# Windowed attention feeding a convolution-gated two-layer network: global rows' scores issued product by product, some elementwise work moved between engines, and a new order of the whole program

## Chip, cores, metric

One NeuronCore of a Trainium2 chip runs the whole problem in a single launch. The metric is device time in microseconds. In the profile PE is TensorE (matmuls), PEld its weight loads, DVE is VectorE, ACT is ScalarE, POOL is GpSimd, and SP is SyncE, which here only issues DMAs.

## What is computed

```python
# 8 batches, 8 heads, 512 local and 32 global rows, head size 64
k_all = concat([k_g, k_l]); v_all = concat([v_g, v_l])
out_g = softmax(0.125 * q_g @ k_all.T) @ v_all           # global rows see all rows
s_ll  = where(|i - j| <= 32, 0.125 * q_l @ k_l.T, -1e9)  # local rows: window of 32 ...
s_lg  = 0.125 * q_l @ k_g.T                              # ... and the global rows
out_l = softmax(concat([s_lg, s_ll])) @ concat([v_g, v_l])
x = concat([out_g, out_l]) as [8 batches, 544 rows, 512]
h = relu(x @ w_in)                                       # 512 -> 1024
c = 3-tap convolution of h along the rows, weights conv_w
out = (h * sigmoid(c)) @ w_out                           # 1024 -> 512
```

## The kernel before

**Attention.** Two heads share the 128 partitions. For each of the 32 pairs of heads, `SC` makes the scores of both (32 products of 32 by 128 on line 258, fp32), and then each head goes alone through: `MA` on VectorE (mask added in PSUM, line 288; row maximum, line 289), `NM` (the maximum scaled, line 238 or 240), `EX` on ScalarE (four exponentials with their sums, line 301), `NS` on VectorE (reciprocal of the sums, lines 317 and 318), `NP` (division of the probabilities, lines 324 to 326) and `TD` on VectorE (32 by 32 transposes, line 311). `PV` multiplies by the values (line 352), `UA` copies the result out of PSUM (line 357), `XW` writes it to a DRAM tile `row` (line 363). Once per batch come the global rows: `G` (24 products on line 282), `GM`, `GE`, `GN`, `GS` (softmax), `GT` and `GC` (transposes and their copies), `GP`, `GO`, `GW`.

`G` is what the change rewrites. For each of four pairs c it makes a product of 384 columns, one of 128 and one of 32, each for the two halves j of the partitions (one head in each half). The pair c fixes the 32 output partitions, c * 32 to c * 32 + 32. The rewritten loop has the same 24 products. In the trace each fp32 product of this kind leaves two matmul records.

**The network.** The 4360 columns of `row` (8 batches of 545) are cut into nine chunks of 484 or 486 columns. For each chunk, `XR` reads four tiles back (line 370), `XH` and `XL` split each into a high part (ScalarE cast, line 205) and a low part (a subtraction, line 208) that suit TensorE's fp32r format. `Z` makes one of eight hidden tiles with 12 products (line 468; three for each of the four x tiles in turn: high, low, high). Each hidden tile is then worked through `RE` (relu, line 476), `C1` (first tap, line 240 when GpSimd does it), two more taps `Ca`, `Cb` on VectorE (line 487), `TH` (tanh, line 494), `GG` (line 498), and again a split into `GH` (cast, line 205) and `GL` (difference, line 208). `O` makes four output tiles with two times 12 products each (line 522), `OE` copies one out, `ST` stores it. A chunk can begin only when the attention of its batch is written and read back.

**Weights.** `w_in` and `w_out` come as 64-bit floats in eight pieces of 1 MB and are turned into fp32 bit by bit: `WA` on ScalarE (line 107), `WC` on VectorE (four instructions, lines 114, 115, 118, 192), `WH` on ScalarE (high part), `WL` on VectorE (low part, line 208).

**What sets the order.** Nothing in the program is issued in the order in which it is written here. A planner (`plan`, `in_time`, `arranged`) gives each step a cost per engine and a due time from the tables `POS`, `POS0`, `POS1` and `TIME`, lists all steps by engine, and `emit` issues them in that order; each engine then runs its own list strictly in order and waits by semaphores. `ENG0` says which engine does a step in the first phase (attention of batches 0 and 1, chunk 0, weights), `ENG` which does it later: "a" is ScalarE, "v" VectorE, "p" GpSimd. The pools' sizes are in `SLOTS`: eight PSUM banks, four tiles of keys, two hidden tiles `h` and two `t`.

Of the kernel before, what the change touches and what calls it, by code (L numbers as in the profile page):

```python
# [64 lines left out]
def attn_moe(ctx: ExitStack, tc: tile.TileContext, qk_d, vw_d, qg_d, w_in_d, w_out_d, cw_d, out_d):  # L65
    nc = tc.nc
# [196 lines left out]
    def G(n):  # L263
# [302 lines left out]
    LQ=40.87, LG=215.93, LV=-243.12, S=107.44, M=-70.51, E=5.13, NS=-78.62, NM=29.46, P=56.84, UA=-17.62,  # L566
    XW=130.55, XR=1.62, NP=66.53, TD=36.03, XH=3.06, XL=-78.47, G=116.57, GM=-316.88, GE=52.46, GN=-126.8,
    GS=36.17, GT=-9.45, GC=-378.84, GP=142.18, GO=60.71, GW=-40.85, PZ=150.79, RE=268.18, C1=145.08, Ca=-140.4,
    Cb=-113.5, TH=59.26, GG=-47.92, GH=-6.62, GL=-138.03, Oa=147.2, Ob=58.82, OE=35.95, ST=218.68, WD=203.65,
    WA=218.1, WC=-74.47, WH=335.66, WL=135.18,  # L570
# [8 lines left out]
POS1 = dict(
    LQ=-63.39, LG=301.35, LV=-335.85, S=193.3, M=77.03, E=20.47, NS=-248.75, NM=-259.8, P=113.29, UA=-43.88,  # L580
    XW=-158.89, XR=-54.07, NP=-38.76, TD=-137.17, XH=-242.78, XL=-129.5, G=-35.21, GM=-113.52, GE=137.51,
    GN=-160.66, GS=-99.25, GT=71.36, GC=-144.02, GP=-27.71, GO=-126.33, GW=45.2, PZ=-196.53, RE=160.59,
    C1=-347.5, Ca=-48.32, Cb=3.66, TH=302.11, GG=61.24, GH=-381.31, GL=-125.69, Oa=6.05, Ob=-16.32, OE=-249.32,
    ST=-157.23, WD=-338.43, WA=368.5, WC=-177.51, WH=182.59, WL=368.35,
# [3 lines left out]
    A0=131.07, R0=-90.01, A1=-373.5, R1=272.56, A2=429.96, R=151.66, PER=64.94, T0=274.61, Z0=-174.31,  # L588
    O0=267.42, OR0=-83.25, T1=275.17, ZR=-32.34, OD=-0.43, OR=-1.06, END=285.22,
# [8 lines left out]
def cost(key, e):  # L598
# [380 lines left out]
```

## Time and profile before

| | us |
|---|---|
| median of 3 runs | 592.79 |
| lowest and highest run | 589.4, 593.7 |
| the profiled execution | 589.3 |
| its span, first to last instruction | 587.5 |

The span is what the views of the profile divide up; 1.8 us of the execution's time lie around it. Every duration below comes from this one execution. Busy times count an engine's instructions, not its waits; the chain of waits says at each moment what the last instruction was waiting for.

### The profile page before, as it was taken

How to read it: one execution, taken by the hardware profiler on the slowest of the kernel's cores; microseconds unless marked ns; L12 is line 12 of the kernel's file. 1: busy time of each engine (PE TensorE's matmuls, PEld its weight loads, DVE VectorE, ACT ScalarE, POOL GpSimd, SP SyncE). 2: the span in 40 equal slices, each digit the busy share in tenths (PEclk: the TensorE clock that was granted, in tenths of full speed). 3: DMA queues.
4: the chain of work that ended last, by engine and by line, in shares of the span. 5: the costliest groups of instructions: out<-in, count | busy, mean ns of one | idle time of the engine just before them, and what ended most of it. 6: DMA issues, size and time to landing. Idle time of an engine off the chain costs nothing.

```text
span 587.5 us, 19573 instructions
## 1 busy us (share of the span) xinstructions
PE 541.6 (92%) x8208; PEld 449.7 (77%) x8208; DVE 406.5 (69%) x846; ACT 391.3 (67%) x1296; POOL 65.4 (11%) x113
## 2 busy tenths in 40 slices
PE   4573599999997999999999999999999999999997
PEld 3362377878786878787888788878888888888886
DVE  4689899999775648876868665758667864552560
ACT  4944896877574888788649965897579753432431
POOL 3000111111120001100200110011100101110110
PEclk9596599999998999999999999999999999999999
DMA  8769662740427416711556027703310230111101
GB/s 352 288 242 304 260 213 79 222 125 35 126 89 203 178 40 175 232 66 39 151 152 223 17 68 198 259 18 120 92 36 29 97 122 0 52 51 35 34 2 67
DMA packets 34984, 74.75 MB, mean 127 GB/s; under 512 B 9808, under 2 KB 21584, under 8 KB 33872
## 3 DMA queue, kind: packets, MB, share of 16 engines
q1 hardware_dynamic: 34896, 73.50, 38.3%
q8 instruction: 64, 1.05, 0.7%
q14 instruction: 24, 0.20, 0.1%
HBM read 55.65 MB, written 17.84 MB: 125 GB/s over the span
## 4 chain that ended last, share of the span: by engine, by line
PE 83%; DVE 7%; issue 5%; DMA 2%; ACT 2%; SPq 1%; POOL 0%; DVEq 0%; ACTq 0%; POOLq 0%
PE ps_h L468 32%; PE ps_o L522 32%; PE ps_v L352 7%; PE psg L282 5%; PE ps_s L258 4%; PE go L438 2%; DMA qk<-qk 1%; ACT pr L301 1%; PE gt L423 1%; DMA raw<-w_out 1%; DVE t L487 1%; DVE negm L289 1%; DVE wt L118 1%; DVE xl L208 1%; DVE nt L205 1%
## 5 line engine op out<-in xcount | busy, mean ns | idle before, releaser
L468 PE MATMUL ps_h<-xh,w_in 128*128 128x486 f32 (+1 forms) x576 | 191.4, 394 | 10.4 <-ACT pr L301 10.1
L522 PE MATMUL ps_o<-g,w_out 128*128 128x484 f32 (+1 forms) x864 | 200.1, 385 | 0.1
L522 PEld LDWEIGHTS ps_o<-g,w_out 128*128 128x128 f32 x864 | 162.3, 190 | 28.4 <-issue 1.6
L468 PEld LDWEIGHTS ps_h<-xh,w_in 128*128 128x128 f32 x576 | 110.2, 191 | 32.5 <-ACT pr L301 10.9
L487 DVE SCALAR_TENSOR_TENSOR t<-h,cw,t 128x484 f32<-128x484 f32 (+1 forms) x144 | 102.5, 721 | 34.6 <-POOL t L240 33.7
L468 PE MATMUL ps_h<-xl,w_in 128*128 128x486 f32 (+1 forms) x288 | 112.0, 389 | 3.1 <-DVE xl L208 3.1
L240 POOL TENSOR_SCALAR t<-h,cw 128x484 f32<-128x484 f32 (+1 forms) x72 | 57.7, 802 | 435.9 <-ACT h L476 307.1
L301 ACT ACTIVATE pr<-ps_s,negm 128x128 f32<-128x128 f32 x256 | 90.3, 378 | 1.8 <-POOL negm L240 1.3
L324 ACT ACTIVATE pr<-pr,sums 128x128 f32<-128x128 f32 x256 | 80.5, 407 | 2.9 <-DVE sums L317 2.0
L498 DVE SCALAR_TENSOR_TENSOR t<-t,h 128x484 f32<-128x484 f32 (+1 forms) x72 | 48.9, 685 | 26.3 <-ACT t L494 26.1
L352 PEld LDWEIGHTS ps_v<-pt,vf 32*64 32x64 f32 x3328 | 48.8, 133 | 21.0 <-issue 14.9
L468 PEld LDWEIGHTS ps_h<-xl,w_in 128*128 128x128 f32 x288 | 55.0, 191 | 12.1 <-DVE xl L208 4.0
L352 PE MATMUL ps_v<-pt,vf 32*64 32x64 f32 (+3 forms) x3328 | 53.8, 245 | 10.8 <-issue 10.3
L476 ACT ACTIVATE h<-ps_h 128x486 f32<-128x486 f32 (+1 forms) x72 | 42.0, 583 | 27.2 <-PE ps_h L468 25.5
L208 DVE TENSOR_TENSOR g<-t,g 128x484 fp32r<-128x484 f32 (+1 forms) x72 | 47.5, 666 | 15.6 <-ACT g L205 14.8
L494 ACT ACTIVATE t<-t 128x484 f32<-128x484 f32 (+1 forms) x72 | 43.6, 612 | 20.1 <-DVE t L487 20.0
L301 ACT ACTIVATION_READ_ACCUMULATOR pr<-ps_s,negm 128x1 f32 x256 | 55.9, 219 | 0.0
L205 ACT CAST g<-t 128x484 fp32r<-128x484 f32 (+1 forms) x72 | 42.9, 600 | 16.0 <-DVE t L498 15.6
L311 DVE STREAM_TRANSPOSE pt<-pr 128x512 f32<-128x512 f32 x64 | 43.3, 695 | 14.8 <-ACT pr L324 12.6
L258 PE MATMUL ps_s<-qk 64*32 64x128 f32 x2048 | 39.5, 295 | 14.7 <-issue 9.3
L258 PEld LDWEIGHTS ps_s<-qk 64*32 64x32 f32 x2048 | 31.9, 113 | 21.5 <-issue 12.8
L289 DVE TENSOR_REDUCE negm<-ps_s 128x4 f32<-128x512 f32 x64 | 44.3, 692 | 3.3
(63 smaller groups left out, 388.0 us busy)
## 6 DMA issues: line engine op xcount, KB each, us to landing
qk<-qk SPq DMA_DIRECT2D x32, 704.0 KB, 5.8
vf<-vw SPq DMA_DIRECT2D x32, 448.0 KB, 4.8
row<-nt SPq DMA_DIRECT2D x32, 256.0 KB, 4.1
xl<-row SPq DMA_DIRECT2D x24, 243.0 KB, 4.0
raw<-w_in SPq DMA_DIRECT2D x4, 1024.0 KB, 11.5
raw<-w_out SPq DMA_DIRECT2D x4, 1024.0 KB, 8.3
xl<-row SPq DMA_DIRECT2D x8, 244.0 KB, 3.3
out<-o SPq DMA_DIRECT2D x4, 242.0 KB, 2.1
```

The source lines that it names most:

```text
L205: nc.scalar.copy(out=out, in_=in_) if choice(key) == "a" else eng(key).tensor_copy(out=out, in_=in_)
L208: eng(key).tensor_tensor(out=out, in0=in0, in1=in1, op=ALU.subtract)
L240: nc.gpsimd.tensor_scalar(out=out, in0=in_, scalar1=by, scalar2=0.0, op0=ALU.mult, op1=ALU.add)
L258: nc.tensor.matmul(heads[n + j]["s"][b * SG : (b + 1) * SG, t].rearrange("p (a b k) -> p a b k", a=2, b=2), lhsT=qk[rows, at : at + SG], r ...
L289: nc.vector.tensor_reduce(out=st["m"], in_=st["s"], axis=mybir.AxisListType.X, op=ALU.max)
L301: nc.scalar.activation(out=st["p"][:, t, :], in_=st["s"][:, t, :], func=AF.Exp, scale=SCALE, bias=st["m"][:, t : t + 1], accum_out=two["r" ...
L324: nc.scalar.activation(out=p[:, t], in_=p[:, t], func=AF.Copy, scale=r[:, t : t + 1])
L352: nc.tensor.matmul(x, lhsT=v, rhs=p, start=k == 0, stop=k == len(work[j, b]) - 1)
L468: nc.tensor.matmul(st["z"][:, 0:n], lhsT=w[:, ft, ct, :], rhs=x, start=i == 0, stop=i == 3 * NCT - 1)
L487: nc.vector.scalar_tensor_tensor(out=st["t"], in0=st["h"][:, k : k + n], scalar=cw[:, 3 * ft + k : 3 * ft + k + 1], in1=st["t"], op0=ALU.m ...
L498: nc.vector.scalar_tensor_tensor(out=t, in0=t, scalar=1.0, in1=h, op0=ALU.add, op1=ALU.mult)
L522: nc.tensor.matmul(ps, lhsT=w[:, mt, ft, :], rhs=g, start=ft + i == 0, stop=ft == NFT - 1 and i == 2)
```

## The change

Three things change. The products of `G` come in another order: first all 384-column ones over the four pairs, then all of 128 columns, then all of 32, so that neighbours differ in their output partitions. Steps change engine: in the first phase `NP` goes from ScalarE to GpSimd, `NM` from GpSimd to ScalarE, `C1` from GpSimd to ScalarE, `UA`, `GS`, `GO` and `OE` from VectorE to ScalarE, `GC` from ScalarE to VectorE; later `C1` goes from GpSimd to ScalarE, `XL` from VectorE to GpSimd, `GH` and `OE` from ScalarE to VectorE. And the tables that set the order are replaced, with some of the planner's costs.

```diff
@@ G
-        for c in range(4):
-            k = heads[first + 2 * c]["qk"]
-            keys = k[:, SL:].rearrange("p (a x) -> p a x", a=4)
-            parts = (
-                ("s0", slice(0, 3 * SG), keys[:, :, 0 : 3 * SG]), ("s0", slice(3 * SG, P), keys[:, :, 5 * SG : 6 * SG]),
-                ("s1", None, k[:, QK - SG : QK]),
-            )
-            for name, at, x in parts:
+        parts = (("s0", slice(0, 3 * SG), 0, 3 * SG), ("s0", slice(3 * SG, P), 5 * SG, SG), ("s1", None, 6 * SG, SG))
+        for name, at, x, w in parts:
+            for c in range(4):
+                keys = heads[first + 2 * c]["qk"][:, SL:].rearrange("p (a x) -> p a x", a=4)
                 for j in range(2):
                     rows, out = slice(j * D, (j + 1) * D), g[j][name][c * SG : (c + 1) * SG]
                     if at:
-                        out = out.rearrange("p (a x) -> p a x", a=4)[:, :, at]
-                    nc.tensor.matmul(out, lhsT=qg[n // H][rows, c, :], rhs=x[rows], start=True, stop=True)
+                        out, k = out.rearrange("p (a x) -> p a x", a=4)[:, :, at], keys[rows, :, x : x + w]
+                    else:
+                        k = keys[rows, 3, x : x + w]
+                    nc.tensor.matmul(out, lhsT=qg[n // H][rows, c, :], rhs=k, start=True, stop=True)
@@ engines
 ENG = dict(
-    GC="a", GO="a", NP="a", XH="a", XL="v", NM="a", RE="a", C1="p", GH="a", GL="v", OE="a", UA="a", GS="a",
+    GC="a", GO="a", NP="a", XH="a", XL="p", NM="a", RE="a", C1="a", GH="v", GL="v", OE="v", UA="a", GS="a",
 ENG0 = dict(
-    GC="a", GO="v", NP="a", XH="a", XL="v", NM="p", RE="a", C1="p", GH="a", GL="v", OE="v", UA="v", GS="v",
+    GC="v", GO="a", NP="p", XH="a", XL="v", NM="a", RE="a", C1="a", GH="a", GL="v", OE="a", UA="a", GS="a",
@@ order (all entries of POS, POS0, POS1 and TIME; two lines shown)
-    A0=131.07, R0=-90.01, A1=-373.5, R1=272.56, A2=429.96, R=151.66, PER=64.94, T0=274.61, Z0=-174.31,
+    A0=-198.68, R0=57.8, A1=68.22, R1=-82.84, A2=94.4, R=59.02, PER=78.97, T0=-127.27, Z0=-72.43, O0=42.3,
@@ planner's costs (ns): a difference on GpSimd, G, NP on GpSimd
-        return 150 + n * 22 // 10, 180 + n * 22 // 10
+        return 60 + n * 27 // 10, 90 + n * 27 // 10
-        ... G=pe(1200) ... (1250, 1300) if e == "p"
+        ... G=pe(1150) ... (1060, 1100) if e == "p"
```

On TensorE the global scores of the first batch stood so before; `psg_482` and `psg_484` are the large score banks of the two halves, `psg_483` and `psg_485` the small ones, and 32x4x96 is a product of 384 columns:

```order
L282 MATMUL psg_482<-qk,qgf 32x4x96
L282 MATMUL psg_484<-qk,qgf 32x4x96
L282 MATMUL psg_482<-qk,qgf 32x4x32
L282 MATMUL psg_484<-qk,qgf 32x4x32
L282 MATMUL psg_483<-qk,qgf 32x32
L282 MATMUL psg_485<-qk,qgf 32x32
L282 MATMUL psg_482<-qk,qgf 32x4x96
L282 MATMUL psg_484<-qk,qgf 32x4x96
L282 MATMUL psg_482<-qk,qgf 32x4x32
L282 MATMUL psg_484<-qk,qgf 32x4x32
```

In the changed kernel the first twelve of the 24 are these, with `psg_374` and `psg_376` for the large banks:

```order
L280 MATMUL psg_374<-qk,qgf 32x4x96
L280 MATMUL psg_376<-qk,qgf 32x4x96
L280 MATMUL psg_374<-qk,qgf 32x4x96
L280 MATMUL psg_376<-qk,qgf 32x4x96
L280 MATMUL psg_374<-qk,qgf 32x4x96
L280 MATMUL psg_376<-qk,qgf 32x4x96
L280 MATMUL psg_374<-qk,qgf 32x4x96
L280 MATMUL psg_376<-qk,qgf 32x4x96
L280 MATMUL psg_374<-qk,qgf 32x4x32
L280 MATMUL psg_376<-qk,qgf 32x4x32
L280 MATMUL psg_374<-qk,qgf 32x4x32
L280 MATMUL psg_376<-qk,qgf 32x4x32
```

Before, six products in a row wrote the same 32 output partitions; now only two do, and eight products of one size cover all four groups of partitions and both halves.

On VectorE, between the third and the fourth low part `xl` of chunk 0, there stood before (scores `ps_s`, their maxima `negm`):

```order
L208 TENSOR_TENSOR xl<-xl,xh 128x486
L288 TENSOR_TENSOR ps_s<-ps_s,mask 128x8x32
L289 TENSOR_REDUCE negm<-ps_s 128x4
L288 TENSOR_TENSOR ps_s<-ps_s,mask 128x8x32
L289 TENSOR_REDUCE negm<-ps_s 128x4
L317 TENSOR_SCALAR sums<-sums 128x4
L318 RECIPROCAL sums<-sums 128x4
L288 TENSOR_TENSOR ps_s<-ps_s,mask 128x8x32
L289 TENSOR_REDUCE negm<-ps_s 128x4
L208 TENSOR_TENSOR xl<-xl,xh 128x486
```

And now, with `wt` a piece of the weights and `pt` the transposed probabilities:

```order
L208 TENSOR_TENSOR xl<-xl,xh 128x486
L309 STREAM_TRANSPOSE pt<-pr 128x512
L315 TENSOR_SCALAR sums<-sums 128x4
L316 RECIPROCAL sums<-sums 128x4
L114 TENSOR_SCALAR wt<-wt 128x1024
L115 TENSOR_SCALAR wt<-wt 128x1024
L118 SCALAR_TENSOR_TENSOR wt<-raw,wt 128x1024
L192 SCALAR_TENSOR_TENSOR wt<-raw,wt 128x1024
L208 TENSOR_TENSOR xl<-xl,xh 128x486
```

A fifth piece of weights has come ahead of the last low part, and all but three of the second batch's eight mask-and-maximum steps have gone behind it; counted over the list from the first piece of weights on, five pieces and three such steps stand ahead of it now, four pieces and eight steps did before.

On the DMA queue, where chunk 4 is read back after the last values of batch 4 were written, there stood before (`row<-nt` writes attention, `row<-og` the global rows, `xl<-row` reads a tile of the chunk, `out<-o` stores, `vf` and `qk` load values and keys):

```order
L450 DMA row<-og_127 128x4x33
L370 DMA xl<-row 128x486
L230 DMA vf<-vw 128x896
L363 DMA row<-nt 128x512
L536 DMA out<-o 128x121
L536 DMA out<-o 128x362
L370 DMA xl<-row 128x486
```

And now:

```order
L448 DMA row<-og_127 128x4x33
L230 DMA vf<-vw 128x896
L361 DMA row<-nt 128x512
L368 DMA xl<-row 128x486 x2
L223 DMA qk<-qk 128x1408 x2
L534 DMA out<-o 128x182
```

The last read of the chunk has moved ahead of the stores and the third read has moved behind the last write.

## Rows read from the trace of the kernel before

**Rows 1.** The page: the span, busy time of each engine, TensorE's busy tenths and granted clock in 40 equal slices, and the chain that ended last by engine and line.

```profile
span 587.5 us, 19573 instructions
PE 541.6 (92%) x8208; PEld 449.7 (77%) x8208; DVE 406.5 (69%) x846; ACT 391.3 (67%) x1296; POOL 65.4 (11%) x113
...
PE   4573599999997999999999999999999999999997
...
PEclk9596599999998999999999999999999999999999
...
PE 83%; DVE 7%; issue 5%; DMA 2%; ACT 2%; SPq 1%; POOL 0%; DVEq 0%; ACTq 0%; POOLq 0%
```

**Rows 2.** Stretches of the span: start and end, length, then busy us and instructions of TensorE, VectorE, ScalarE and so on, the granted clock (1.00 is full), the DMA engines' share and GB/s.

```profile
50.00:60.00 10.00, 2.39 (x80) 1.93 (x80) 9.74 (x11) 3.27 (x4) 0.00 (x0) 0.50 0.90 317
...
90.00:100.00 10.00, 10.00 (x124) 7.79 (x124) 9.56 (x20) 4.37 (x8) 2.20 (x2) 1.00 0.10 34
...
250.00:300.00 50.00, 49.59 (x718) 41.37 (x717) 36.14 (x77) 37.39 (x125) 6.52 (x8) 1.00 0.32 89
```

**Rows 3.** What TensorE waited for after 95 us: total us, times, longest.

```profile
PE ps_s L258 <- issue: 2.7, 1, 2.7
PE ps_v L352 <- issue: 1.8, 4, 0.8
PE ps_h L468 <- ACT pr L301: 1.1, 1, 1.1
PE go L438 <- issue: 1.0, 1, 1.0
```

**Rows 4.** TensorE in order of time around the first hidden tiles: start, length, line, tiles, count, and in brackets the idle time before and what ended it.

```profile
62.48 0.77 PE L468 MATMUL ps_h<-xh,w_in 128*128 128x486 f32 x1 [8.99 <-ACT pr L301]
...
71.33 0.77 PE L468 MATMUL ps_h<-xl,w_in 128*128 128x486 f32 x1 [2.05 <-DVE xl L208]
...
75.95 3.16 PE L282 MATMUL psg<-qk,qgf 64*32 64x384 f32 x48
79.04 0.49 PE L468 MATMUL ps_h<-xh,w_in 128*128 128x486 f32 x1
```

**Rows 5.** TensorE in order of time (columns as in rows 4): the global scores of the first batch and of the last, and two pairs' scores, the latter two with the row that follows.

```profile
25.25 5.37 PE L282 MATMUL psg<-qk,qgf 64*32 64x384 f32 x48
...
390.10 3.16 PE L282 MATMUL psg<-qk,qgf 64*32 64x384 f32 x48
393.19 0.49 PE L468 MATMUL ps_h<-xh,w_in 128*128 128x486 f32 x1
...
244.84 2.06 PE L258 MATMUL ps_s<-qk 64*32 64x128 f32 x128
246.83 10.78 PE L522 MATMUL ps_o<-g,w_out 128*128 128x484 f32 x48
```

**Rows 6.** ScalarE and VectorE in the first 76 us by line and shape: count, busy us, mean ns of one, idle time before.

```profile
L301 ACT ACTIVATE pr<-ps_s,negm 128x128 f32<-128x128 f32 x56 | 19.7, 382 | 1.3 <-POOL negm L240 1.3
L324 ACT ACTIVATE pr<-pr,sums 128x128 f32<-128x128 f32 x44 | 13.7, 411 | 1.3 <-DVE sums L317 0.7 <-DVE sums L318 0.5
...
L289 DVE TENSOR_REDUCE negm<-ps_s 128x4 f32<-128x512 f32 x16 | 11.1, 692 | 1.4
L288 DVE TENSOR_TENSOR ps_s<-ps_s,mask 128x256 f32<-128x256 f32 x16 | 6.7, 420 | 7.1 <-PE ps_s L258 7.1
L311 DVE STREAM_TRANSPOSE pt<-pr 128x512 f32<-128x512 f32 x10 | 6.6, 686 | 1.2 <-ACT pr L324 1.2
L118 DVE SCALAR_TENSOR_TENSOR wt<-raw,wt 128x1024 uint32<-128x1024 uint32 x5 | 6.1, 1227 | 0.2
L192 DVE SCALAR_TENSOR_TENSOR wt<-raw,wt 128x1024 uint32<-128x1024 uint32 x5 | 6.1, 1225 | 0.2
...
L205 DVE COPY nt<-ps_v 128x128 f32<-128x128 f32 x16 | 3.6, 279 | 0.1
L115 DVE TENSOR_SCALAR wt<-wt 128x1024 uint32<-128x1024 uint32 x5 | 3.5, 694 | 0.2
L114 DVE TENSOR_SCALAR wt<-wt 128x1024 f32<-128x1024 f32 x5 | 3.4, 676 | 0.0
```

**Rows 7.** VectorE in order of time: the first piece of weights begins, and the fourth low part of chunk 0.

```profile
36.82 0.68 DVE L114 TENSOR_SCALAR wt<-wt 128x1024 f32<-128x1024 f32 x1
...
70.62 0.65 DVE L208 TENSOR_TENSOR xl<-xl,xh 128x486 fp32r<-128x486 f32 x1
```

**Rows 8.** GpSimd's work by line over the whole run: count, ns min/median/max, first and last start.

```profile
L240 POOL TENSOR_SCALAR t<-h,cw x72: 662/673/2060, 76.3 to 566.1; 128x484 f32<-128x484 f32 x56, 128x486 f32<-128x486 f32 x16
L240 POOL TENSOR_SCALAR negm<-negm x16: 192/193/539, 8.5 to 70.8; 128x4 f32<-128x4 f32 x16
```

**Rows 9.** The boundary to chunk 4, in order of time: TensorE's last values of batch 4 and its first product of chunk 4, the DMA queue's write and last read, ScalarE's cast, VectorE's low part.

```profile
297.60 0.59 PE L352 MATMUL ps_v<-pt,vf 32*64 32x96 f32 x33 [0.41 <-issue]
...
312.03 0.38 PE L468 MATMUL ps_h<-xh,w_in 128*128 128x486 f32 x1
...
304.96 0.33 SPq L370 DMA_DIRECT2D xl<-row  x1
...
308.44 0.60 ACT L205 CAST xh<-xl 128x486 fp32r<-128x486 f32 x1 [2.24 <-DMA xl<-row]
...
309.16 0.66 DVE L208 TENSOR_TENSOR xl<-xl,xh 128x486 fp32r<-128x486 f32 x1
```

More of the change, by code (lines that the diff above doesn't have):

```diff
@@ L565 @@
 POS = dict(
[L566 to L570, printed above, removed]
+    LQ=-49.5, LG=-130.06, LV=145.65, S=48.52, M=-20.73, E=46.17, NS=41.72, NM=2.35, P=199.02, UA=2.52, XW=26.25,
@@ L571 @@
+    XR=30.89, NP=-10.4, TD=-37.85, XH=-55.05, XL=65.97, G=-220.2, GM=25.92, GE=-42.92, GN=74.33, GS=93.36,
+    GT=249.93, GC=-252.01, GP=10.64, GO=-47.21, GW=1.48, PZ=-31.03, RE=9.54, C1=-8.2, Ca=-9.15, Cb=7.83,
+    TH=-112.69, GG=-54.54, GH=1.05, GL=66.32, Oa=3.54, Ob=112.43, OE=-51.88, ST=-26.21, WD=-241.88, WA=-63.83,
+    WC=-137.59, WH=8.34, WL=-34.22,
 )
 POS0 = dict(
-    LQ=-27.84, LG=-411.01, LV=36.06, S=-155.18, M=-333.78, E=-66.6, NS=111.14, NM=-450.56, P=115.25, UA=203.11,
-    XW=49.58, XR=114.87, NP=104.11, TD=7.74, XH=-63.01, XL=-237.35, G=50.35, GM=395.61, GE=154.22, GN=-34.91,
@@ L575 @@
-    GS=76.45, GT=270.97, GC=1.63, GP=187.97, GO=494.66, GW=-467.94, PZ=-194.98, RE=-426.94, C1=-56.31,
-    Ca=-303.83, Cb=41.19, TH=98.9, GG=12.61, GH=94.13, GL=-375.53, Oa=379.49, Ob=55.01, OE=29.28, ST=-343.47,
-    WD=185.44, WA=217.46, WC=-44.54, WH=-30.1, WL=166.88,
+    LQ=-172.39, LG=118.97, LV=-96.95, S=164.17, M=-141.48, E=121.44, NS=200.21, NM=-78.79, P=-70.58, UA=35.6,
+    XW=116.03, XR=-65.24, NP=68.41, TD=-19.4, XH=-333.62, XL=120.97, G=19.81, GM=-59.33, GE=69.29, GN=-189.16,
+    GS=-203.52, GT=19.33, GC=-19.41, GP=48.7, GO=133.67, GW=-30.43, PZ=-234.87, RE=189.44, C1=116.91, Ca=7.6,
@@ L578 @@
+    Cb=-98.65, TH=54.29, GG=-103.7, GH=-134.29, GL=24.26, Oa=-128.77, Ob=-38.25, OE=-49.61, ST=58.33,
+    WD=-136.03, WA=63.13, WC=85.87, WH=45.1, WL=26.14,
 )
 POS1 = dict(
[L580 to L583, printed above, removed]
@@ L584 @@
-    ST=-157.23, WD=-338.43, WA=368.5, WC=-177.51, WH=182.59, WL=368.35,
+    LQ=129.3, LG=206.98, LV=-76.91, S=253.45, M=17.93, E=97.33, NS=125.74, NM=-63.61, P=169.56, UA=-17.57,
+    XW=32.06, XR=-188.95, NP=-25.82, TD=-25.2, XH=-85.35, XL=-176.04, G=17.59, GM=-48.53, GE=2.57, GN=228.84,
+    GS=-88.42, GT=88.79, GC=-47.4, GP=-229.77, GO=39.95, GW=-116.62, PZ=109.67, RE=34.73, C1=-95.95, Ca=86.35,
+    Cb=90.16, TH=152.84, GG=-54.59, GH=-53.84, GL=116.96, Oa=-105.74, Ob=148.18, OE=-118.88, ST=76.46,
@@ L585 @@
+    WD=-83.79, WA=-105.54, WC=-274.06, WH=-63.4, WL=3.4,
 )
 TIME = dict(
[L588 to L589 removed]
+    A0=-198.68, R0=57.8, A1=68.22, R1=-82.84, A2=94.4, R=59.02, PER=78.97, T0=-127.27, Z0=-72.43, O0=42.3,
+    OR0=29.71, T1=-1.11, ZR=118.43, OD=111.78, OR=-16.45, END=-22.97,
 )
```

4 lines of the change are left out of this document (2 added, 2 removed).

## The prediction

> **What bounds the kernel now.** I read the page first. TensorE is busy for 92% of the span and the chain that ended last lies on it for 83%; its row of tenths shows where it is not: the first six of the 40 slices, with a granted clock of 0.5 in several of them [rows 1]. The view by stretches says the same in numbers. From 50 to 60 us TensorE works 2.39 of 10 us, at 0.50 of the clock (the 1.2 GHz level), while VectorE works 9.74; from 250 to 300 us TensorE works 49.59 of 50 at the full clock, with VectorE at 36.14 and ScalarE at 37.39 [rows 2]. So there are two regimes. Early, the weights' conversion and the first softmaxes bound the kernel, on VectorE above all. From about 76 us on TensorE's own work does: after 95 us its waits come to 2.7 + 1.8 + 1.1 + 1.0 = 6.6 us in all [rows 3]. In the second regime a microsecond taken off TensorE's list is a microsecond of the result; in the first only an earlier start of the stream of hidden tiles counts.
>
> **Term 1: the global scores.** The last batch's 24 products start at 390.10 and the next product at 393.19, so they cost 3.09 us [rows 5]. They leave 48 records, eight each of (384 + 128 + 32) columns, twice: 16 * 544 = 8704 columns, or 2820 columns per us. Two pairs' scores are products of the same kind (64 rows, 32 output partitions, both halves), but issued so that neighbours go to different output partitions: 128 records of 128 columns, 16384 columns, from 244.84 to 246.83, which is 1.99 us or 8230 columns per us [rows 5]. The new order of `G` is that order. At that rate 8704 columns take 1.06 us, a gain of 2.03 us per batch. Bounds: no gain, if the wide products behave otherwise; at best about 0.9 us left, if I take the start out of the 1.99. I take 1.06, because the row is of the same instruction with the same tiles. Seven of the eight stand in the stretch that TensorE bounds (the second batch's starts at 75.95 us [rows 4]): 7 * 2.03 = 14.2 us. The first one, 5.25 us at the low clock [rows 5], now stands before the first values are ready, where TensorE waits anyway; I count it in term 2.
>
> A rule speaks against this. The Trainium skill, "TensorE: Matmul & The Clock Gate", Part 3, says that a weight load overlaps running products only when its group of rows differs. By it, the same half j for the next pair c would still wait, and the gain would be nothing. The two pairs' scores, which change the output partitions within one half, ran at 8230 columns per us against 2820, so the trace speaks against the rule here; I keep it as a rival.
>
> **Term 2: the start.** Two things decide when the first hidden tiles run: when VectorE begins the weights (36.82 us) and when it ends the fourth low part of chunk 0 (70.62 + 0.65 = 71.27) [rows 7]. TensorE waits for that low part at 71.33 [rows 4].
> (a) Before the weights VectorE waits for softmaxes, and these for ScalarE. There a head's exponentials cost 4 * 19.7/56 = 1.41 us and its division 4 * 13.7/44 = 1.25 us [rows 6]. The eight divisions of batch 0, 10.0 us, leave ScalarE. It gets eight scalings of the maxima (at 0.2 us, as GpSimd's row has it [rows 8]: 1.6 us), two scalings of the global rows and two copies of values before the first weight (bounded by what it gives as relief, the two copies of transposes: about 1.5 us net). What is left is some 7 us. VectorE's own list before the weights is in the way for part of it, and it must now wait for GpSimd's division: no row shows a two-input step on GpSimd; its one-input step of 484 takes 0.67 us undisturbed and up to 2.06 [rows 8], so 512 with two inputs lie between 0.7 and 2.2; I take 1.2, near the lower end, since VectorE's transposes and small steps leave room there, and it keeps pace with the exponentials' 1.41. I take 5.5 of the 7 us (bounds 2.5 and 7): weights from 31.3 us.
> (b) From there to the fourth low part VectorE's list was four pieces of weights (0.68 + 0.69 + 1.23 + 1.23 = 3.82 each), eight masks and maxima (1.11 each), three copies of values (4 * 0.28 = 1.12 each, less overlaps) and small steps. Now it is five pieces, three masks and maxima, no copies, and one more transpose (0.69) [rows 6]: +3.8 - 5.6 - 2.9 + 0.7 = -4.0 us. The low part would end at 71.3 - 5.5 - 4.0 = 61.8 us. The weights' high parts, the reads of the chunk and of the second batch's last keys come earlier on the DMA queue or have over 10 us to spare.
> (c) What is late next: five masks and maxima and five exponentials of batch 1 (5 * 1.41 = 7 us of ScalarE) have been put behind the low part. They hold PSUM banks and stand between the first hidden tiles' relus, which ScalarE must also do before TensorE may go on, and ScalarE now also has the first taps. GpSimd's divisions of batch 1 meet VectorE's weights there. I give back 2 us (bounds 0 and 7).
> Sum of term 2: -5.5 - 4.0 + 2.0 = -7.5 us (bounds about -11 and 0).
>
> **Term 3: the later stream.** The same products run, in nearly the same number of runs of small products. Per hidden tile ScalarE loses a cast and gains a tap of the same length, and loses four copies per chunk; VectorE gains casts and copies (about 0.4 and 0.65 us) and loses four low parts (0.66): per chunk 8 * 0.4 + 4 * 0.65 - 4 * 0.66 = +3.2 us, on 36.14 of 50 us [rows 2], so it stays near 80% of a chunk's time. Both stay below TensorE: cost nothing. The 6.6 us of late waits [rows 3] belonged to the old order; I count half of them as gone, 3.3, less 0.3 for a few more changes between kinds of products: -3.0 us (bounds 0 and -6.6).
>
> **Term 4: GpSimd's low parts at a chunk's boundary.** A chunk's first tile needs the attention just computed, written and read back. At chunk 4 the last values end at 298.19, the read is issued at 304.96, the cast starts at 308.44, the low part at 309.16, and TensorE came to the chunk at 312.03, 13.8 us after the values [rows 9]. In the new order four output steps and two pairs' scores stand between: 48 products in 10.78 us plus 1.99 [rows 5], 12.7 us; the last low part is used in the eleventh of the twelve products, some 2.2 us later. So it may end 14.9 us after the values. It starts 10.97 us after them (309.16 - 298.19), which leaves 3.9 us for GpSimd. I expect 1.2 to 2.2 [rows 8]: hidden. The read also leaves ahead of the stores now. If that cover is gone, each us beyond 3.9 costs a us at each of eight boundaries.
>
> **Sum.** 589.3 (the profiled execution) - 14.2 - 7.5 - 3.0 = 564.6 us. That execution is at the low end of the runs shown, 3.5 us below their median; I add half of that and forecast a median of 566.5 us.
>
> **Rivals.**
> 1. The start gives nothing back: what leaves ScalarE and VectorE before the low part returns behind it, as waits of TensorE for relus and banks. For it: VectorE was busy 9.56 of 10 us from 90 to 100 us too [rows 2], and its work was only moved. Against it: some of it went to GpSimd, which was busy 11% [rows 1]. Term 2 becomes 0: 566.5 + 7.5 = 574 us.
> 2. The global scores stay at 3.09 us, because products of one half j run one after the other whatever partitions they write. For it: the old order, at 2820 columns per us, overlaps little. Against it: the pairs' scores [rows 5]. 566.5 + 14.2 = 580.7 us.
> 3. Slower: GpSimd's low parts stall every boundary. For it: its longest step took 2.06 us against a median of 0.67 [rows 8], and VectorE will be busy for four fifths of the time, mostly with two-input steps. It decides from 3.9 us per low part; to end 1% slower than now it must take about 8 us, 4.1 beyond the cover, at eight boundaries: 566.5 + 33 = 599 us. Against it: that is four times the longest step seen. The Trainium skill, "SBUF — State Buffer", section on the two separate sides, says that GpSimd and a VectorE step with two inputs in SBUF shut each other out for a whole instruction. By it a low part waits for one such step, which the 2.06 us bears out, and not for eight us.
>
> **How the numbers follow.** Forecast 0.74, rival 1 0.15, rival 2 0.06, rival 3 0.05. The forecast's own range follows from the bounds of terms 2 and 3. The lower end takes terms 2 and 3 at their best: 566.5 - 3.5 - 3.6 = 559, and 3 more for runs as fast as the profiled one or global scores below 1 us: 556. The upper end takes in rival 1 and most of the way to rival 2: 580. A difference of 1% (5.9 us) is about what a measurement of this kernel can tell from no change. Forecast and both first rivals are faster by more than that, by 2.0% at the least; I leave 0.04 for no change (two of these rivals and part of the third together) and 0.04 for slower: 0.92, 0.04, 0.04.
>
> **What would show it.** Right: the 24 products of a batch's global scores take 1.0 to 1.2 us; the fourth low part of chunk 0 ends near 62 us; TensorE is over 98% busy from 100 us to its end; the chain is on TensorE for over 85%. Wrong: global scores near 3 us (term 1); a low part at 62 us but the second batch's global scores not before 76 us, or a TensorE that waits for relus until 110 us (rival 1); waits of the first product of a chunk for GpSimd's `xl` (rival 3).

## The result, and the profile after

The changed kernel takes 569.14 us (median of 4 runs, 568.72 to 570.99), the kernel before 591.15 us beside it (4 runs, 589.4 to 593.7): a ratio of 0.963, 95% interval 0.958 to 0.968. The forecast was 566.5 us, within 556 to 580. The profiled execution took 569.44 us, its span is 567.6 us, 19.9 us below that of before. The total is near the sum that was forecast. Its parts are not: the global scores gave less than was counted on, the start almost nothing, and the later stream three times as much.

The page first, against [rows 1]. TensorE's row began 45735 and then read 9 but for a 7 at the thirteenth slice; now it begins 557458988 and reads 9 from there on (the last slice reads 7 in both). The chain lies on TensorE for 82%, with 11% on VectorE.

```profile
span 567.6 us, 19439 instructions
...
PE 528.4 (93%) x8208; PEld 442.8 (78%) x8208; DVE 431.4 (76%) x876; ACT 377.5 (67%) x1258; POOL 65.1 (11%) x73
...
PE   5574589889999999999999999999999999999997
...
PEclk9676689899999999999999999999999999999999
...
PE 82%; DVE 11%; DMA 3%; ACT 2%; issue 2%; SPq 0%; ACTq 0%; DVEq 0%
```

By stretches, with the columns of [rows 2]: from 50 to 60 us TensorE works 7.01 us instead of 2.39. But from 100 to 120 us, where it worked 19.63 of 20 us before, it now works 15.79. From 250 to 300 us it is never idle. First the two stretches of the kernel before that [rows 2] leaves out, then the changed kernel:

```profile
100.00:110.00 10.00, 9.63 (x334) 8.21 (x332) 9.81 (x27) 9.57 (x22) 0.87 (x1) 1.00 0.86 237
110.00:120.00 10.00, 10.00 (x106) 8.61 (x107) 9.40 (x18) 7.65 (x28) 1.74 (x2) 1.00 0.59 167
```

```profile
50.00:60.00 10.00, 7.01 (x125) 4.72 (x105) 9.76 (x18) 6.37 (x16) 1.55 (x2) 0.67 1.02 413
...
90.00:100.00 10.00, 10.00 (x163) 8.29 (x162) 9.76 (x27) 6.59 (x15) 1.34 (x1) 1.00 0.23 61
100.00:110.00 10.00, 7.92 (x185) 6.10 (x188) 9.86 (x16) 7.74 (x17) 2.07 (x1) 0.83 0.43 124
110.00:120.00 10.00, 7.87 (x321) 7.11 (x306) 7.54 (x11) 6.16 (x17) 1.22 (x1) 1.00 0.46 129
120.00:130.00 10.00, 9.99 (x222) 7.82 (x220) 9.76 (x16) 7.76 (x35) 1.23 (x1) 1.00 0.87 296
...
250.00:300.00 50.00, 50.00 (x966) 42.17 (x966) 38.82 (x85) 36.81 (x125) 5.39 (x4) 1.00 0.47 143
...
130.00:567.60 437.60, 433.38 (x6040) 366.47 (x6038) 317.74 (x650) 289.80 (x968) 38.90 (x33) 1.00 0.32 101
```

TensorE's waits after 95 us, against [rows 3] ("issue" is a wait for which the profile names no releaser). Of these 4.6 us all but 0.4 us lie before 118 us; the late waits of the old order are gone.

```profile
PE ps_v L350 <- issue: 2.2, 2, 1.8
PE ps_o L520 <- ACT pgt L205: 2.1, 1, 2.1
PE go L436 <- issue: 0.3, 1, 0.3
```

TensorE in order of time, for [rows 4, 5, 9]. The 24 products of the global scores start at 379.92 and the next product at 381.05, so they cost 1.13 us where they cost 3.09. The wait for the fourth low part ends at 64.50 instead of 71.33. In the second batch, the values' products wait 1.57 us for VectorE to read the global scores; at 102.8 us TensorE stands still for 2.08 us, and the twelve products behind that hole take 4.36 us, at a granted clock of 0.62, where twelve such take 2.89 us elsewhere (118.30). The first hidden tile of chunk 1 starts at 132.81, that of chunk 4 at 300.43 without a wait.

```profile
64.50 0.77 PE L466 MATMUL ps_h<-xl,w_in 128*128 128x486 f32 x1 [3.42 <-DVE xl L208]
...
74.84 1.21 PE L280 MATMUL psg<-qk,qgf 64*32 64x384 f32 x48
...
80.86 2.27 PE L350 MATMUL ps_v<-pt,vf 32*64 32x128 f32 x100 [1.57 <-DVE pg L387]
...
104.85 4.36 PE L520 MATMUL ps_o<-g,w_out 128*128 128x484 f32 x12 [2.08 <-ACT pgt L205]
...
116.97 0.31 PE L350 MATMUL ps_v<-pt,vf 32*64 32x32 f32 x6 [1.82 <-issue]
...
118.30 2.89 PE L520 MATMUL ps_o<-g,w_out 128*128 128x484 f32 x12
...
132.81 0.38 PE L466 MATMUL ps_h<-xh,w_in 128*128 128x486 f32 x1
...
300.43 0.38 PE L466 MATMUL ps_h<-xh,w_in 128*128 128x486 f32 x1
...
379.92 1.21 PE L280 MATMUL psg<-qk,qgf 64*32 64x384 f32 x48
381.05 0.49 PE L466 MATMUL ps_h<-xh,w_in 128*128 128x486 f32 x1
```

VectorE, for [rows 7]: the weights begin at 32.55 (36.82 before), the fourth low part ends at 63.78 + 0.66 = 64.44 (71.27 before).

```profile
32.55 0.67 DVE L114 TENSOR_SCALAR wt<-wt 128x1024 f32<-128x1024 f32 x1
...
63.78 0.66 DVE L208 TENSOR_TENSOR xl<-xl,xh 128x486 fp32r<-128x486 f32 x1
```

GpSimd's two new kinds of steps (count, ns min/median/max, first and last start), for [rows 8], and the last low part of chunk 4, for [rows 9]: it ends at 298.08, before the first product of the chunk.

```profile
L324 POOL TENSOR_TENSOR pr<-pr,sums x16: 1039/1042/1458, 12.0 to 91.1; 128x512 f32<-128x512 f32 x16
```

```profile
L208 POOL TENSOR_TENSOR xl<-xl,xh x32: 1217/1241/2074, 107.9 to 508.7; 128x486 fp32r<-128x486 f32 x24, 128x488 fp32r<-128x488 f32 x8
```

```profile
296.85 1.23 POOL L208 TENSOR_TENSOR xl<-xl,xh 128x486 fp32r<-128x486 f32 x1 [0.58 <-ACT xh L205]
```

**How far TensorE is.** Below, runs are compared by the work that TensorE has done up to a time: each run of products counts with its length at the full clock and without waits (a hidden tile 2.64, an output step 2.62, a pair's scores 0.90, a pair's values 1.47, the global rows' scores 1.13, transposes 0.55, values 2.40 us; 491.6 us in all). "G alone" is the kernel before with the new order of products in `G`, the first experiment; "NP back" is the changed kernel with the divisions on ScalarE. All in us.

| at | before | G alone | changed | NP back |
|---|---|---|---|---|
| 80 | 25.0 | 27.7 | 32.4 | 26.2 |
| 100 | 41.2 | 43.7 | 48.7 | 40.8 |
| 125 | 64.1 | 64.8 | 66.2 | 58.8 |
| 135 | 72.4 | 73.8 | 75.3 | 65.7 |
| 400 | 310.8 | 319.5 | 330.6 | 320.0 |

The changed kernel is 5.0 us ahead of G alone at 100 us, 1.4 us at 125 us, and 11.1 us at 400 us. So a lead is won at the start, mostly lost between 100 and 125 us, and a larger one is won in the stream.

### The profile page after: what moved, and what is told of

It reads as the page before. It is cut to its first block, busy times and chain, and to the rows that moved or that the text cites. A ratio compares the mean times of both kernels' runs of the same rounds, so it can differ in the third digit from the quotient of the medians.

```text
span 567.6 us, 19439 instructions
## 1 busy us (share of the span) xinstructions
PE 528.4 (93%) x8208; PEld 442.8 (78%) x8208; DVE 431.4 (76%) x876; ACT 377.5 (67%) x1258; POOL 65.1 (11%) x73
## 4 chain that ended last, share of the span: by engine, by line
PE 82%; DVE 11%; DMA 3%; ACT 2%; issue 2%; SPq 0%; ACTq 0%; DVEq 0%
PE ps_o L520 34%; PE ps_h L466 31%; PE ps_v L350 7%; PE ps_s L258 5%; PE go L436 3%; DVE negm L287 2%; DMA qgf<-qg 1%; DVE t L485 1%; DVE pt L309 1%; PE gt L421 1%; PE psg L280 1%; DVE ps_s L286 1%; DVE t L496 1%; DMA qk<-qk 1%; DVE wt L118 1%
## 5 line engine op out<-in xcount | busy, mean ns | idle before, releaser
L485 DVE SCALAR_TENSOR_TENSOR t<-h,cw,t 128x484 f32<-128x484 f32 (+1 forms) x144 | 105.9, 742 | 16.2 <-ACT t L238 15.6
L208 POOL TENSOR_TENSOR xl<-xl,xh 128x486 fp32r<-128x486 f32 (+1 forms) x32 | 43.2, 1353 | 349.2 <-ACT xh L205 349.2
L350 PEld LDWEIGHTS ps_v<-pt,vf 32*64 32x64 f32 x3328 | 50.7, 140 | 20.8 <-issue 12.2
L350 PE MATMUL ps_v<-pt,vf 32*64 32x64 f32 (+3 forms) x3328 | 56.6, 254 | 9.2 <-issue 4.4
L496 DVE SCALAR_TENSOR_TENSOR t<-t,h 128x484 f32<-128x484 f32 (+1 forms) x72 | 51.0, 713 | 16.5 <-ACT t L492 15.5
L322 ACT ACTIVATE pr<-pr,sums 128x128 f32<-128x128 f32 x192 | 60.1, 404 | 0.6 <-DVE sums L316 0.5
L286 DVE TENSOR_TENSOR ps_s<-ps_s,mask 128x256 f32<-128x256 f32 x64 | 26.8, 418 | 38.8 <-PE ps_s L258 38.6
L238 ACT ACTIVATE t<-h,cw 128x484 f32<-128x484 f32 (+1 forms) x72 | 50.5, 703 | 4.8 <-DVE g L208 4.2
L299 ACT ACTIVATION_READ_ACCUMULATOR pr<-ps_s,negm 128x1 f32 x256 | 53.1, 208 | 0.0
L208 DVE TENSOR_TENSOR g<-t,g 128x484 fp32r<-128x484 f32 (+1 forms) x72 | 49.6, 692 | 1.4
```

The lines of the kernel that those rows point to most:

```text
L208: eng(key).tensor_tensor(out=out, in0=in0, in1=in1, op=ALU.subtract)
L238: nc.scalar.activation(out=out, in_=in_, func=AF.Copy, scale=by)
L299: nc.scalar.activation(out=st["p"][:, t, :], in_=st["s"][:, t, :], func=AF.Exp, scale=SCALE, bias=st["m"][:, t : t + 1], accum_out=two["r" ...
L322: nc.scalar.activation(out=p[:, t], in_=p[:, t], func=AF.Copy, scale=r[:, t : t + 1])
L350: nc.tensor.matmul(x, lhsT=v, rhs=p, start=k == 0, stop=k == len(work[j, b]) - 1)
L485: nc.vector.scalar_tensor_tensor(out=st["t"], in0=st["h"][:, k : k + n], scalar=cw[:, 3 * ft + k : 3 * ft + k + 1], in1=st["t"], op0=ALU.m ...
```

## The experiments

**The global scores alone, and all but them.** Before with the new order of products in `G`, and the changed kernel with the old one:

```diff
-        for c in range(4):
-            ...
-            for name, at, x in parts:
+        for name, at, x, w in parts:
+            for c in range(4):
```

> The kernel before with only the products of G in the new order; engines and order of everything else as before. Theory: a batch's 24 products fall from 3.09 to 1.14 us and TensorE bounds the run from 76 us on, so seven batches give 7 * 1.95 = 13.7 us: about 577 us where before has 591 (ratio 0.977), and the late waits of TensorE (6.6 us after 95 us) stay or grow. Rival: TensorE's time saved comes back as waits for VectorE and ScalarE, which the old order was fitted to: 583 us or more (ratio above 0.986).

> The changed kernel with the products of G in the old order, all else as changed. Theory: plus 13 to 14 us on the changed kernel's 569: 582 to 584 us, so the new order and engines alone are worth about 7 to 8 us against before. Rival: the rest alone is worth nothing, 589 us or more.

G alone: 578.73 us (ratio to before 0.980, 0.974 to 0.987), 11.4 us less than the 590.09 us of the kernel before measured beside it. The old products in the changed kernel: 580.55 us, 11.4 us more than 569.14. The two agree, so the edit is worth 11.4 us in either order (13 to 14 us were expected), and all the rest together 9.6 us (11.1 us between the profiled spans, 578.7 and 567.6). The late waits of before stay with G alone; TensorE's, after 130 us:

```profile
PE ps_v L350 <- issue: 2.5, 3, 1.2
PE ps_s L258 <- issue: 2.2, 1, 2.2
PE go L436 <- issue: 0.9, 1, 0.9
PE ps_v L350 <- ACT og L205: 0.3, 1, 0.3
```

**Is VectorE's list the bound of the start?** Without the four bit steps for each of `w_out`'s four pieces (15.3 us of VectorE), in the changed kernel and in the kernel before:

```diff
-        if wpe == 2:
+        if wpe == 2 and i < 4:
```

> The changed kernel without VectorE's four bit steps for the last four pieces of weights (w_out), 4 * 3.8 = 15.3 us of VectorE between 59 and 126 us; the output is then not the reference's. Theory: VectorE (9.7 of 10 us busy from 50 to 110 us) bounds the start, and the 10 us that TensorE loses to waits and low clock between 76 and 118 us mostly go: 7 to 11 us less, 558 to 562 us. Rival: TensorE waits there for ScalarE's exponentials and relus: under 3 us less, 566 us or more.

> The kernel before without VectorE's four bit steps for the last four pieces of weights (w_out), 15.3 us of VectorE between 73 and 146 us; the output is then not the reference's. Theory: the old order put the first output tiles late and TensorE lost only some 3 us after 76 us, so VectorE's work there is covered: 2 to 5 us less, 586 to 589 us. Rival: VectorE bounds the old start as much as the new: 7 us less or more, 584 us or below.

566.08 us and 591.4 us (ratio 1.0015, 0.998 to 1.005): by medians 3.1 us gained in the one, nothing in the other, which missed both expectations. VectorE is busy for 9.7 and more of every 10 us from 50 to 110 us, yet 15.3 us taken off its list, most of them in that stretch, bring 3.1 us, where 7 to 11 were expected; the rival had put it at under 3 us. Busy for all of a stretch was not the same as bounding it.

**Is the quiet stream the order's, or the engines'?** The changed kernel with the later phase's steps back on the old engines, and G alone with these four kinds of steps on the new ones:

```diff
-        return (ENG0 if phase[0] == 0 else ENG)[key]
+        moved = {} if phase[0] == 0 else {'C1': 'p', 'GH': 'a', 'OE': 'a', 'XL': 'v'}
+        return moved.get(key) or (ENG0 if phase[0] == 0 else ENG)[key]
```

```diff
+        moved = {} if phase[0] == 0 else {'C1': 'a', 'GH': 'v', 'OE': 'v', 'XL': 'p'}
```

> The changed kernel with the later phase's four kinds of steps back on the engines of the kernel before (first taps on GpSimd, gate casts and output copies on ScalarE, the hidden tiles' low parts on VectorE); the order of every list as in the changed kernel. Between the kernel before with the new products alone (578.7 us) and the changed kernel (569.1 us) lie some 9.6 us, nearly all after 130 us. Theory, the order: the late waits are gone because of where the runs of small products now stand, whichever engine does the small steps: 568 to 572 us, TensorE's waits after 130 us under 1.5 us in all. Rival, the engines: the lists of ScalarE and VectorE kept TensorE waiting, and moving these four kinds of steps took the waits away: 575 to 580 us, with 3 to 7 us of waits after 130 us.

> The other way round: the kernel before with the new products of the global scores, its own old order, and the four kinds of steps of the later phase on the changed kernel's engines (first taps on ScalarE, gate casts and output copies on VectorE, low parts on GpSimd). Theory, the order: 577 to 582 us, as without the move (578.7 us), the late waits (2.5 + 2.2 + 0.9 us) stay within 2 us; it may be slower by some us, since the old order leaves GpSimd less room for the low part at a chunk's boundary. Rival, the engines: 570 to 574 us, and the late waits fall under 2 us.

572.58 us (569.9 to 574.57) and 583.24 us (ratio to before 0.988, 0.984 to 0.992). With the new order and the old engines TensorE waits 0.2 us after 130 us:

```profile
PE ps_v L351 <- issue: 0.2, 1, 0.2
```

With the old order and the new engines, in the same view, the waits are still there, in the same places:

```profile
PE ps_s L259 <- issue: 3.4, 2, 2.7
PE ps_v L351 <- issue: 2.1, 3, 1.2
PE go L437 <- issue: 0.9, 1, 0.9
PE gt L422 <- ACT pg L239: 0.4, 1, 0.4
PE ps_h L467 <- ACT pr L300: 0.2, 1, 0.2
```

So the late waits go with the order. What the engines add by themselves is smaller than these runs can tell for sure: in the old order they cost 4.5 us by the medians, with runs that spread over 11.2 us, in the new one they give 3.4 us, with runs that spread over 4.7 us. With GpSimd's low parts in the old order TensorE does not wait for one either.

**What are the start's engines worth, in each order?** In the changed kernel, all eight kinds of steps of the first phase back, and the divisions alone (the "NP back" of the table); in G alone, the divisions alone on GpSimd, and all eight moved:

```diff
+        moved = {'GC': 'a', 'GO': 'v', 'NP': 'a', 'NM': 'p', 'C1': 'p', 'OE': 'v', 'UA': 'v', 'GS': 'v'} if phase[0] == 0 else {}
```

```diff
+        moved = {'NP': 'a'} if phase[0] == 0 else {}
```

```diff
+        moved = {'NP': 'p'} if phase[0] == 0 else {}
```

```diff
+        moved = {'GC': 'v', 'GO': 'a', 'NP': 'p', 'NM': 'a', 'C1': 'a', 'OE': 'a', 'UA': 'a', 'GS': 'a'} if phase[0] == 0 else {}
```

> The changed kernel with the first phase's eight kinds of steps back on the engines of the kernel before (divisions and copies of transposes on ScalarE, scalings of maxima and first taps on GpSimd, copies of values, output copies and scalings of the global rows on VectorE), every list in the new order. What the fourth low part of chunk 0 gained (71.3 to 64.4 us) was mostly lost again before the second chunk (1.4 us left). Theory, the gain was swallowed behind the low part, so the start's engines are worth little: the low part ends 3 to 8 us later (67 to 72 us), but the time is 569 to 573 us. Rival, the moved engines give the whole low part's gain to the result: 574 to 579 us.

> The changed kernel with the first batches' divisions alone back on ScalarE; all else as changed. Theory (ScalarE before the weights was what VectorE waited for): VectorE's first weight starts 3 to 7 us later than 32.6 us; of that 0 to 3 us reach the end, since a later low part finds its followers in time: 569 to 572 us. Rival 1: ScalarE's list is the bound from 50 to 110 us as well, so the eight or sixteen divisions (1.25 us each) come out in full there: 576 to 585 us. Rival 2: the division's engine made no difference, the first weight stays within 1 us of 32.6 us, and the new order of VectorE's list alone brought it forward: 568 to 570 us.

> The kernel before with the new products of the global scores (578.7 us alone) and the first phase's divisions on GpSimd; all lists in the old order. In the new order the divisions' engine was worth 11.3 us (580.5 against 569.1 us). Theory A: the divisions hold up ScalarE's list in either order, so the engine gives about as much here, 566 to 572 us, and the new order of the start by itself costs what it does not show. Theory B: the order and the engine belong together; in the old order VectorE's list before the first weight does not wait for the divisions, and the move gives 0 to 3 us: 575 to 580 us. Slower than 581 us would say that GpSimd's division comes too late for the steps behind it in the old order.

> The same with all eight kinds of steps of the first phase on the changed kernel's engines (divisions on GpSimd; scalings of the maxima and of the global rows, first taps, copies of values and output copies on ScalarE; copies of transposes on VectorE), in the old order. Theory A (the engines alone relieve the start): 564 to 572 us. Theory B (only the new order makes use of them): 575 to 582 us. In the new order the eight moves together were worth 13.0 us, the division 11.3 of them.

Changed kernel: 582.16 us with all eight back, above both expectations, and 580.47 us with the divisions alone back, where rival 1 had put it. So in the new order the divisions' engine is worth 11.3 us, and my expectation that a later low part would cost 0 to 3 us fell. With the divisions on ScalarE, that engine is full (9.97 and 9.32 of 10 us from 80 to 100 us; 9.11 and 6.59 in the changed kernel) and VectorE waits 4.7 us for it there, where no wait shows in the changed kernel; VectorE's first weight starts 6.5 us later:

```profile
80.00:90.00 10.00, 8.07 (x150) 5.86 (x151) 7.08 (x23) 9.97 (x36) 0.00 (x0) 1.00 0.56 210
90.00:100.00 10.00, 8.59 (x129) 6.51 (x111) 7.89 (x18) 9.32 (x29) 0.00 (x0) 1.00 0.29 114
```

```profile
39.08 0.67 DVE L114 TENSOR_SCALAR wt<-wt 128x1024 f32<-128x1024 f32 x1
```

In the old order the same move gives nothing: 579.2 us against 578.73, the first weight 1.0 us earlier (34.34 against 35.30), and at 125 us the work done is the same to a tenth (64.8 us). All eight: 583.23 us, 1 us above theory B's range. So order and engines belong together, as theory B had it. The new order with the old engine is 6.0 us behind G alone at 125 us (58.8 against 64.8); the move brings 7.4 us by then (66.2).

**What loses the lead between 100 and 125 us?** The high parts of `w_out`'s last three pieces on GpSimd, then that together with the cut above:

```diff
-        cp("WH", parts(i)[0], f(wf[i]) if wpe == 2 else drop(raw[i]))
+        if i < 5:
+            cp("WH", parts(i)[0], f(wf[i]) if wpe == 2 else drop(raw[i]))
+        else:
+            nc.gpsimd.tensor_copy(out=parts(i)[0], in_=f(wf[i]))
```

> The changed kernel with the high parts of the last three pieces of the output weights (three casts of 128x1024 on ScalarE, 1.04 us each, at 100.0, 112.1 and 126.2 us) on GpSimd. By work done on TensorE the changed kernel is 7 us ahead of the kernel before at 80 to 100 us and 2 us at 125 us. Theory: the lead is lost because these casts stand on ScalarE's list and wait there for VectorE's conversion, with the copies and relus that TensorE waits for behind them (the wait of 2.1 us for a copy of transposes at 102.8 us, then the low clock): without them 564 to 567 us, the wait at 102.8 us under 0.5 us. Rival: the two engines' lists are late there with or without the casts, or GpSimd's cast makes VectorE's conversion longer in turn: 568 to 572 us, with the wait of 2 us or another in its place.

> The changed kernel without VectorE's four bit steps for each of the output weights' four pieces (15.3 us of VectorE; the weights are then not the reference's), and with the high parts of the last three pieces on GpSimd instead of ScalarE (3.1 us of ScalarE). Alone the first gave 3.1 us (566.1) and left 1.1 of the 2.1 us wait for the copy of transposes, with ScalarE's list without a gap for 6 us before it; the second gave nothing (571.9) and left 2.8 us, with ScalarE in gaps that ended on VectorE. Theory: the two lists hold the lead of the start jointly, each steps in when the other is relieved: the wait falls under 0.5 us and the time to 562 to 565 us. Rival: with both relieved something else is late there (the values' copies, the order of the small products): 565.5 to 568 us.

571.93 us: the theory that ScalarE's casts hold the lead fell, and the wait did not shrink (2.8 us, 2.1 in the changed kernel). TensorE's waits from 95 to 130 us:

```profile
PE ps_o L523 <- ACT pgt L208: 2.8, 1, 2.8
PE ps_v L353 <- issue: 1.8, 1, 1.8
PE go L439 <- issue: 0.2, 1, 0.2
```

Beside GpSimd's cast of 1.47 us (99.24 to 100.71) a VectorE step that took 0.72 us at 99.10 took 1.24 us, and between 99 and 104 us three more gaps of 0.3 to 0.4 us on ScalarE's list ended on VectorE. GpSimd's cast, and VectorE's two rows:

```profile
99.24 1.47 POOL L200 CAST w_out<-wt 128x1024 fp32r<-128x1024 f32 x1 [7.02 <-DVE wt L192]
...
99.10 0.72 DVE L488 SCALAR_TENSOR_TENSOR t<-h,cw,t 128x484 f32<-128x484 f32 x1
...
99.99 1.24 DVE L488 SCALAR_TENSOR_TENSOR t<-h,cw,t 128x484 f32<-128x484 f32 x1
```

The Trainium skill, "SBUF — State Buffer", section "SBUF: two separate sides", says that such a pair of steps shuts each other out for a whole instruction; the trace agrees in kind: the step lost 0.52 us, of the 0.72 us that were left of the cast when it started.

With both lists relieved: 565.2 us, between the two expectations and 0.9 us below the cut alone, which the runs cannot tell apart. The wait for the copy of transposes fell to 0.7 us, while the wait inside the values' products stayed (TensorE, 95 to 130 us):

```profile
PE ps_v L353 <- issue: 2.1, 1, 2.1
PE ps_o L523 <- ACT pgt L208: 0.7, 1, 0.7
PE go L439 <- issue: 0.2, 1, 0.2
```

From 100 to 125 us TensorE does 18.8 us of work there, 17.5 in the changed kernel, and 21.1 in G alone. So the loss mostly stays although both lists are shorter; two thirds of what the cuts gain is there at 100 us already (51.2 us done against 48.7, then 70.0 against 66.2 at 125 us). That points to where the small products stand in that stretch.

**What the waits without a releaser are.** The wait of 1.8 to 2.1 us inside the values' products is an "issue" wait, and so are most of the late waits of the old order. The traces hold more on them, in DMA queue 8, which the page calls an instruction queue: it carries 64 packets of 16 KB, most of them in flight for about 1 us.

```profile
q8 instruction: 64, 1.05, 0.8%
```

The wait of 2.73 us in the kernel before ends at 182.15, 1.38 us after such a packet has landed (180.77); the 1.82 us in the changed kernel end at 116.97, 1.38 us after one (115.59). So it is with all 48 "issue" waits over 0.25 us after 95 us in the 14 profiled executions: each ends 1.2 to 1.6 us after the landing of a packet, and counted in the instructions that the trace lists for TensorE, weight loads included, each stands 193 or 194 behind 256 times the number of packets landed. TensorE was waiting for its own instructions there; no run changed the packets, so this rests on the count and the times alone. Small products use the instructions up fastest. The longest run of them without a hidden tile or an output step, 352 products (values, global rows' values, values, scores), stands once in each order: at 173 us in the kernel before, with the hole of 2.73 us, and at 109 us in the changed kernel, with the waits of 0.3 and 1.8 us. So part of what the start lost and the stream won is one and the same run, moved. Runs of 288 such products stand in both orders, with waits of 0.8 and 1.0 us before and 0.4 us at most now; why they fare better now was not isolated.

## Why the prediction was right or wrong

The number came out (2.6 us off) because errors offset each other: terms 1 and 2 were counted too large, term 3 too small. That the sum came so near is luck.

| term | forecast | measured, between profiled runs |
|---|---|---|
| 1, global scores | -14.2 | -8.8 (span 587.5 to 578.7); -11.4 by medians |
| 2, the start | -7.5 | -0.7 |
| 3, the later stream | -3.0 | -10.5; -8.9 by medians (9.6 less 0.7) |
| 4, chunk boundaries | 0 | 0 |

The profiled execution of G alone took 580.53 us, 1.8 us more than the median of its runs; in the first figures that takes from term 1 and adds to term 3.

**Term 1: the mechanism right, the count too large.** The batch takes 1.13 us, forecast 1.06 from the pairs' scores. The starts in the trace say what held the old loop up. There the two halves of a pair start together (390.10), and the next pair 0.68 us later; now all eight products of 384 columns start within 0.05 us (379.92 to 379.96). The halves share their output partitions and start together in either order, and a product of 384 columns of the next pair started 0.01 us behind one of 128 columns (390.774, 390.780), so the mix of sizes was not it: what waited was the same half writing to the same 32 output partitions. Rival 2, by which one half waits whatever it writes, is out. The Trainium skill, "TensorE: Matmul & The Clock Gate", Part 3, says that a weight load overlaps running products only when its group of rows differs, by which, taken alone, the batch would have stayed at 3.09 us in either order; the row of 1.13 us disagrees. The step that failed is "Seven of the eight stand in the stretch that TensorE bounds". Five do: 5 * (3.09 - 1.13) = 9.8 us. The second and third batch's stand between 75 and 99 us, where most of what TensorE saves was still swallowed: G alone is 2.5 us ahead at 100 us and 0.7 us at 125 us, and with the old products put back into the changed kernel its first tile of chunk 1 starts at 134.35 instead of 132.81. With these 0.7 and 1.5 us the five batches' 9.8 us come to 10.5 and 11.3 us, near the 11.4 of the medians.

**Term 2: the step that failed is (c), "I give back 2 us".** Steps (a) and (b) were nearer: the weights from 32.55 us (forecast 31.3), the low part at 64.4 us (61.8), so 6.8 us of the 9.5 came. GpSimd's division takes 1.04 us (1.2). Then the first hidden tile of chunk 1 starts at 132.81, with three output steps and a pair's scores more done by then, 3 * 2.62 + 0.90 = 8.8 us; at equal work that is 124.0 us, against 124.7 in G alone and 125.43 before. The start gave 0.7 us of its own; 4.3 us of the 5.0 us lead went back (forecast 2, bounds 0 and 7): 2.1 + 0.3 + 1.8 us of waits and a low clock from 100 to 120 us. For this term rival 1, at 0.15, gave the size. Its cause holds for half: the 2.1 us are an output step that reads nothing of the transposes and yet waited until ScalarE had copied them, so by the program a wait for a PSUM bank. No wait was for a relu, and the other 2.1 us are waits for instructions. The order's own part was not seen at all: I took the new engines as a gain on the old order, and there they are worth nothing.

**Term 3: the waits went as forecast, but the size was wrong and their cause was not seen.** "I count half of them as gone": nearly all were, and one of them had cost more than its wait. In the kernel before, a wait of 2.73 us at 179 us is followed by twelve output products in 4.46 us instead of the 2.89 us that twelve take at 118.30 in the changed kernel:

```profile
178.78 0.64 PE L258 MATMUL ps_s<-qk 64*32 64x128 f32 x24
182.15 0.86 PE L258 MATMUL ps_s<-qk 64*32 64x128 f32 x40 [2.73 <-issue]
182.94 4.46 PE L522 MATMUL ps_o<-g,w_out 128*128 128x484 f32 x12
```

In that stretch the granted clock is 0.60, part of it at the 1.2 GHz level; the other row is the changed kernel's stretch behind its hole of 2.08 us:

```profile
183.00:187.30 4.30, 4.30 (x14) 3.36 (x12) 4.10 (x8) 1.38 (x3) 0.00 (x0) 0.60 0.72 204
```

```profile
104.90:109.10 4.20, 4.20 (x12) 3.08 (x12) 4.10 (x7) 2.84 (x9) 1.25 (x1) 0.62 0.28 88
```

So this one hole cost 2.7 + 1.6 us; behind the others of the late stream there (0.4 to 1.1 us) twelve products took 2.9 us, as usual. From the first tile of chunk 1 to the end, TensorE spends 23.2 us more than the counted work in G alone and 12.7 us in the changed kernel: 10.5 us. Of these, 6.0 us are waits (6.4 against 0.4), and about 3.1 us are the slow products behind two holes of G alone (2.19 and 1.22 us). The excess of 12.7 us is 13.2 us with the late engines put back and 13.2 us with the divisions back, so this part hangs on neither.

**Term 4 and rival 3.** Hidden, as forecast: 1.22 to 2.07 us per low part (expected 1.2 to 2.2), no wait of TensorE for one in the later stream.

Of the signs named ahead, three held: global scores of 1.0 to 1.2 us, TensorE over 98% busy from 100 us to its end (7.92 + 7.87 + 9.99 + 433.38 us of 463.8, 99%), no wait for low parts at boundaries. Two did not: the low part near 62 us (64.4), and the chain at over 85% on TensorE (82%).

Two readings of the prediction were slightly off, without weight for the rest: the row of tenths is low in the first five slices, not six, and 564.6 us plus half of 3.5 is 566.35 us.

## What to carry to other kernels

Small products that use a part of the array are best issued so that those of one row half write to different output partitions one after the other (1.13 us instead of 3.09 for the 24 here), and the gain counts only in the stretches that TensorE bounds; find the first of these by the work done, not by when an engine starts to look busy. A hole in TensorE's work can cost more than its length, so look at the products behind it. Where the profile names no releaser for a wait in a run of small products, look whether an instruction packet landed just before it ended. In a list-scheduled start, what a step's engine is worth can only be told together with the order: the same move was worth 11.3 us in one order and nothing in the other.

## What the runs showed of the hardware that was not expected

A hole in TensorE's work was sometimes followed by products at a low clock: twelve output products took 4.46 us after 2.73 us of waiting, 4.36 us after 2.08 us and, in G alone, 4.47 us after 1.22 us, against 2.8 to 2.9 us. After the 1.82 us at 115 us in the changed kernel they took 2.89 us, so the length of the hole alone did not decide.

TensorE's instructions came in packets of 16 KB, 256 instructions each by the count above, and where runs of small products used them up, it stood still for up to 2.8 us until 1.2 to 1.6 us after the next one had landed.

GpSimd's two-input step on 512 columns took 1.04 us in the median (1.46 at the most), below the 1.2 us that I had taken; the low parts of 486 columns took 1.22 us at the least and 2.07 us at the most.
